# Softmax attention followed by a leaky-ReLU feed-forward: score chunks of 128 keys with a shared rest, loaded and scored one unit at a time

## The chip, the core and the metric

The kernel runs on one core of a Trainium2 chip. The core has TensorE (PE, matrix products; PEld is its weight load), VectorE (DVE), ScalarE (ACT), GpSimd (POOL) and SyncE (SP), each with its own in-order queue, and 16 DMA engines. Here SP and POOL issue nearly all transfers: SP the transposing DMAs and the stores, POOL the loads. The metric is the device time of one execution in microseconds (us); lower is better.

## The reference

Attention over 8 batches and 12 heads, 448 tokens, head size 64; the heads are joined to rows of 768; then two weight matrices with a leaky ReLU between them.

```
scores = scale * np.matmul(q, k.transpose(0, 1, 3, 2))        # 448 x 448 for each head
scores = scores - np.max(scores, axis=-1, keepdims=True)
attn   = np.exp(scores); attn = attn / (np.sum(attn, axis=-1, keepdims=True) + 1e-09)
x      = np.matmul(attn, v)                                     # then heads joined: 3584 x 768
h      = x @ w_in                                               # 768 -> 2048
out    = np.maximum(0.01 * h, h) @ w_out                        # 2048 -> 768
```

## The kernel before, in words

A **unit** is two heads of one batch: 48 units, six to a batch. For a unit, the keys lie on partitions in four chunks of 112. A **score chunk** (`scores`, lines 280-290) is two matmuls of 64 rows by 448 queries, one for each head, into one of three PSUM slots; `expo` (line 294) turns both heads' scores of that chunk into exponentials in one ACT instruction of 112 x 896. A **burst** (`burst`, lines 822-832) is three chunks in a row, six matmuls for the three slots, whatever units they belong to. **Rows** (`rows`, lines 793-816) are the product of a unit's exponentials with its values: 4 query blocks x 4 key chunks x 2 heads = 32 matmuls of 65 columns (64 values and a column of ones that gives the softmax's sum), then a reciprocal and a multiplication on DVE (lines 808, 809), then a transposing DMA of x on SP into `xT` (`x_transposes`, line 251).

Queries and keys come as pairs of units by one POOL load for q, k and v each (`load_soft`, line 143, 112 partitions x 4 heads x 256 elements, cast to bf16 on the way), are copied by POOL into `qkb` (`cast`, line 172; values into `v`, line 174), and from unit 15 on are turned by a transposing DMA on SP (`turn`, line 251) into `qkT`, which has four buffers. `qkb` and `e` have three buffers, `v` four.

The feed-forward works on seven stretches of tokens (`cuts`, line 41). For stretch i, `hidden` (lines 458-536, matmuls at line 483) makes the first layer by a scheme with mixed operands (`x_mix`, made on DVE at line 430 from `xT`, and `w_in_mix`), with partial sums kept in the pool `c`; `second(i)` (lines 941-973, matmuls at lines 555 and 620) makes the second layer. Between the steps of `second(i)` the function `place` (lines 885-939) puts bursts and rows, by a small model of when ACT is done and the slots are free (0.8 us for each exponential). `plan` (line 882) says how many bursts go into each `second(i)`, and `need` (line 44) which units must have had their rows before `hidden(i + 1)`; the DVE steps of `x_mix` for the next stretch are set in 7.0 model microseconds after the rows that they need. Two banks `g` take the second layer's sums, and DVE moves them out (lines 560, 563, 623). `advance` (lines 771-791) issues, in each step, the next turn on SP, the next casts on POOL and every second time a load.

All order is fixed when the kernel is built: every engine runs its list in order and waits on semaphores.

Of the kernel before, what the change touches and what calls it, by code (L numbers as in the profile page):

```python
# [16 lines left out]
def kernel(  # L17
# [19 lines left out]
    NW = DM // 2  # L37
    NU = B * HP
    scale = 1.0 / float(D) ** 0.5

# [8 lines left out]
    w_pool = ctx.enter_context(tc.tile_pool(name="weights", bufs=1))  # L49
    ld_pool = ctx.enter_context(tc.tile_pool(name="ld", bufs=2))  # L50
    cast_pool = ctx.enter_context(tc.tile_pool(name="cast", bufs=3))
    v_pool = ctx.enter_context(tc.tile_pool(name="vones", bufs=1))
# [29 lines left out]
    PL = D + 2  # L82
    v_sb = [v_pool.tile([SC, 2, NSC, VL], BF16, name=f"v{i}") for i in range(NV)]

    NE = 3
    EL = 2 * NSC * S
    e_sb = [exp_pool.tile([SC, EL + P - SC], BF16, name=f"e{i}") for i in range(NE)]


    NQ = 4  # L90
    QL = 2 * S
    qkT = [qk_pool.tile([P, QL + P - SC], BF16, name=f"qkT{i}") for i in range(NQ)]

# [30 lines left out]
    for t, n in ((h_mix, 2), (w_in_mix, 9), (w_mix, 9)):  # L124
        t = t.rearrange("p x k n -> p (x k n)")
        for j in range(n):
            rooms.append(t[:SC, ts(j, 4 * NSC * D)].bitcast(F32).rearrange("p (h so d) -> p h so d", h=2, so=NSC))

    def room(x):

        return rooms.pop(0) if rooms else ld_pool.tile([SC, 2, NSC, D], F32, name="f" + "qkv"[x])

    def half(t, i=None):

        t = t.rearrange("p h so d -> p (h so d)").bitcast(BF16)
        t = t.rearrange("p (u h so d) -> p u h so d", u=2, h=2, so=NSC)
        return t if i is None else t[:, i]

    def load_soft(u, n, which):
        b, hp = divmod(u, HP)  # L140
        for x in which:
            t = room(x)
            nc.gpsimd.dma_start(
                out=half(t)[:, :n].rearrange("p u h so d -> p (u h) (so d)"),
                in_=(q, k, v)[x][b, 2 * hp:2 * hp + 2 * n].rearrange(
                    "h (p so) d -> p h (so d)", so=NSC),
            )
            for i in range(n):
                raw.setdefault(u + i, {})[x] = half(t, i)

    def load_one(u, x, queue):
        b, hp = divmod(u, HP)
        t = room(x)
# [10 lines left out]
    def cast(u, parts=(0, 1, 2), by=nc.gpsimd.tensor_copy):  # L164
        if u >= NU:
            return
        for x in parts:
            f = raw[u].pop(x)
            if x < 2 and u not in qk_sb:
                qk_sb[u] = cast_pool.tile([SC, 2, NSC, 2, D], BF16, name="qkb")  # L170
            if x < 2:
                by(qk_sb[u][:, x].rearrange("p so h d -> p h so d"), f)  # L172
            else:
                by(v_sb[u % NV][:, :, :, :D], f)  # L174
    w_steps = []
# [56 lines left out]
    for t in e_sb:  # L232
        nc.vector.memset(t[:, EL:], 0.0)
    for t in qkT:
        nc.vector.memset(t[:, QL:], 0.0)
    fast = nc.vector.tensor_copy
# [12 lines left out]

    def turn(dst, src):  # L250
        nc.sync.dma_start_transpose(out=dst.rearrange("p (c s) -> p c s", s=SC), in_=src)
# [9 lines left out]
    def transposes(u, bank=None):  # L261
        if u >= min(NPE, NU):
            return
        for parts in ((1,), (0,)) if u == 0 else ((0, 1),):
            tr = turn_tile(bank)
            for i in parts:
                for so in range(NSC):
                    nc.tensor.transpose(  # L268
                        tr[:, i, ts(so, SC)], qk_sb[u][:, i, so], ident[:SC, :SC]
                    )  # L270
# [7 lines left out]
    sc_t = {}  # L278

    def scores(u, c):  # L280
        ps = next_slot()
        t = qkT[u % NQ]
        sc_t[u, c] = ps
        for j in range(2):
            nc.tensor.matmul(  # L285
                ps[:, j, :S],
                t[j * D:(j + 1) * D, S + c * SC:S + c * SC + P],
                t[j * D:(j + 1) * D, :S],
                start=True, stop=True,
            )  # L290

    def expo(u, c):
        e = e_sb[u % NE][:, :EL].rearrange("p (j c s) -> p j c s", j=2, c=NSC)
        nc.scalar.activation(e[:, :, c, :], sc_t.pop((u, c))[:SC, :, :S], AX.Exp, scale=scale)  # L294

    def pv(u, j, bank=None):
# [4 lines left out]
        for qc in range(NSC):  # L301
            for c in range(NSC):
                at = (j * NSC + c) * S + qc * SC
                nc.tensor.matmul(  # L304
                    ps[:, qc, :D + 1], e[:, at:at + P], vt[:, j, c, :D + 1],
                    start=(c == 0), stop=(c == NSC - 1),
                )
# [458 lines left out]
    chunk = 4 * HP + 3  # L766
    rows_done = HP
    to = {"pe": HP + 2, "turn": NPE, "q": HP + 4, "cast": HP + 4, "v": HP + 4, "load": [HP + 8] * 3}
    tick = 0

    def advance():
        nonlocal tick
        tick += 1
        u = to["turn"]
        if u < min(NU, chunk // NSC + NQ, to["cast"]):
            dma_transposes(u)
            to["turn"] += 1
# [15 lines left out]
    def rows():  # L793
# [3 lines left out]
        ps = next_slot()[:, :, :NSC * PL].rearrange("p j (q d) -> p j q d", q=NSC)  # L797
        for j in range(2):
            for qc in range(NSC):
                for c in range(NSC):  # L800
                    at = (j * NSC + c) * S + qc * SC
                    nc.tensor.matmul(  # L802
                        ps[:, j, qc, :D + 1], e[:, at:at + P], vt[:, j, c, :D + 1],
                        start=(c == 0), stop=(c == NSC - 1),
                    )
        x_t[u] = x_pool.tile([SC, NSC, 2, D], BF16, name="x")
        rec = r_pool.tile([SC, 2, NSC, 1], F32, name="rec")
        nc.vector.reciprocal(rec, ps[:SC, :, :, D:D + 1])  # L808
        nc.vector.tensor_mul(  # L809
            x_t[u].rearrange("p q j d -> p j q d"), ps[:SC, :, :, :D], rec.to_broadcast([SC, 2, NSC, D])  # L810
        )
        if u in X_PE:
# [9 lines left out]
    def burst(lazy=0):  # L822
        nonlocal chunk
        todo = [divmod(chunk + x, NSC) for x in range(3) if chunk + x < NU * NSC]
        assert rows_done > todo[-1][0] - NE and turned(todo[-1][0]) and to["v"] > rows_done
        for a, c in todo:
# [54 lines left out]

    plan = [9, 8, 8, 8, 8, 5, 0]
    model = {"now": 0.0, "act": 0.0, "free": {}, "ready": {}}

    def place(i, want, soon=0, full=True, calm=True, first=False, lazy=0, keen=NU, cap=NU):
# [3 lines left out]
        while True:  # L889
            settle_x(model["now"])  # L890
            now = model["now"]
            last = divmod(chunk + 2, NSC)[0]
            blocked = rows_done <= min(last, NU - 1) - NE
            u = rows_done
            whole = u < chunk // NSC
            at = [free.get(id(x), 0.0) for x in slots]
            u = to["pe"]
            if full and max(want, soon) > done and u <= min(last, NPE - 1) and state == 0:
# [4 lines left out]
                continue  # L903
            if want > done and state < 2 and turned(last) and not blocked and len(slots) == 3 and all(
                x <= now + 0.05 + 0.2 * j for j, x in enumerate(at)
# [8 lines left out]
                for x, t in enumerate(order[:chunk - start]):  # L914
                    model["act"] = max(model["act"], now + 0.45 + 0.2 * x) + 0.8
                    free[id(t)] = model["act"] + (0.3, 0.15 + 0.5 * (lazy > 1), 0.15 + 0.5 * lazy)[x]
                    if (start + x) % NSC == NSC - 1:
                        ready[(start + x) // NSC] = model["act"] + 0.1
                model["now"] = now + 0.78
                continue  # L920
            u = to["pe"]
            if first and full and state == 0 and u < min(NPE - 1, to["cast"] - 1) and u <= chunk // NSC + 1 and model["act"] <= now + 0.6:
# [6 lines left out]
            if calm and whole and not (lazy and late) and at[0] <= now + 0.05 and ready.get(u, 0) <= now + 0.05 and (  # L929
                u <= (chunk + 5) // NSC - NE or u < keen  # L930
            ) and u < cap:
# [9 lines left out]
    def second(i):  # L941
# [27 lines left out]
        assert left == 0 or chunk == NU * NSC, (i, left)  # L969
        assert i + 1 == NR or rows_done >= need[i + 2], (i, rows_done)  # L970
# [65 lines left out]
```

## Time and profile before

| | us |
|---|---|
| three runs: median (lowest to highest) | 388.05 (386.12 to 391.76) |
| the profiled execution's own time | 387.23 |
| its span (first to last instruction) | 385.4 |
| PE busy | 375.7 (97%) |
| ACT busy | 264.2 (69%) |
| DVE busy | 234.1 (61%) |
| POOL busy | 141.7 (37%) |

The span is what the profile divides its shares by; the 1.8 us by which the execution's own time is longer lie around it. An engine's busy time counts its own instructions; matmuls are pipelined and their ends modelled, so what one really costs is read from start to start of neighbours, not from its mean duration. In the answers below a line of the timeline gives the start, the time to the end of the last one, engine, line, operation, tiles and how many; in brackets how long the engine sat idle before it and what released it.

### The profile page before, as it was taken

The page shows a single profiled execution, that of the slowest core. Times are in us where ns is not written, and L with a number is a line of the kernel's source. Part 1 is how long each engine was busy: PE and PEld are TensorE (multiplying, and loading weights), DVE is VectorE, ACT ScalarE, POOL GpSimd, SP SyncE. Part 2 cuts the span into 40 slices and gives each one's busy share as a digit, 9 for nine tenths or more (in the row PEclk, how much of TensorE's full clock was granted, in tenths as well). Part 3 has the DMA queues.
Part 4 walks back from the last instruction along what each step waited for, and adds up shares of the span by engine and source line. Part 5 has one row for each costly group of instructions (what it writes and reads, how often), then busy time and mean ns, then how long its engine had stood idle before and what let it go on. Part 6 is the DMA issues. An engine that isn't in the chain of part 4 may idle for free.

```text
span 385.4 us, 10023 instructions
## 1 busy us (share of the span) xinstructions
PE 375.7 (97%) x4095; PEld 260.0 (67%) x4095; DVE 234.1 (61%) x488; ACT 264.2 (69%) x391; POOL 141.7 (37%) x223
## 2 busy tenths in 40 slices
PE   8999989999999999999999999999999999999995
PEld 3664646866488655886568865678655895668753
DVE  3663656775666746757459574566745665474753
ACT  5996874865768777687775877767776687717700
POOL 5998660764655443440436304353042100000000
PEclk9999999999999999999999999999999999999999
DMA  8999999899989948991499913999229600330022
GB/s 160 181 195 202 179 193 204 95 135 179 166 149 124 153 72 156 194 156 26 65 182 189 138 26 54 181 173 164 29 46 180 144 13 3 107 80 27 3 83 82
DMA packets 93278, 47.09 MB, mean 122 GB/s; under 512 B 51888, under 2 KB 89904, under 8 KB 93232
## 3 DMA queue, kind: packets, MB, share of 16 engines
q0 software_dynamic: 37536, 22.24, 45.5%
q1 hardware_dynamic: 55056, 23.66, 32.0%
q8 instruction: 32, 0.52, 0.6%
q10 hardware_dynamic: 640, 0.56, 0.5%
q14 instruction: 14, 0.11, 0.1%
HBM read 45.61 MB, written 11.01 MB: 147 GB/s over the span
## 4 chain that ended last, share of the span: by engine, by line
PE 90%; ACT 4%; DMA 2%; DVE 1%; issue 1%; ACTq 0%; DVEq 0%
PE g L555 30%; PE g L483 14%; PE sc L483 14%; PE sc L285 10%; PE sc L802 10%; PE g L366 3%; ACT e L294 3%; PE g L620 3%; PE g L662 2%; DMA xT<-x 2%; PE g L268 1%; DMA hmix<-in_k_dram 1%; PE g L304 1%; PE sc L366 1%; PE g L331 0%
## 5 line engine op out<-in xcount | busy, mean ns | idle before, releaser
L294 ACT ACTIVATE e<-sc 112x896 bf16<-112x896 f32 x192 | 162.7, 920 | 47.7 <-PE sc L285 47.7
L555 PEld LDWEIGHTS <-h 128*128 128x128 bf16 x632 | 57.2, 98 | 45.4 <-issue 13.7
L555 PE MATMUL g<-w_out_sb,h 128*128 128x384 bf16 x416 | 81.0, 326 | 0.0
L472 ACT ACTIVATE h<-c 128x512 bf16<-128x512 f32 (+1 forms) x72 | 43.5, 611 | 25.8 <-DVE c L498 17.4
L483 PEld LDWEIGHTS <-w_in_sb 128*128 128x128 bf16 x576 | 54.3, 98 | 5.9
L285 PE MATMUL sc<-qkT 64*128 64x448 bf16 x384 | 50.0, 355 | 1.4 <-ACT e L294 0.6
L172 POOL COPY qkb<-fq 112x512 bf16<-112x512 bf16 x38 | 25.4, 668 | 68.8 <-DMA qkT<-qkb 33.7
L174 POOL COPY v<-fv 112x512 bf16<-112x512 bf16 x38 | 24.6, 660 | 69.2 <-PE sc L802 69.2
L802 PEld LDWEIGHTS <-e 112*128 112x128 bf16 x1344 | 46.2, 97 | 5.0 <-ACT e L294 0.8
L802 PE MATMUL sc<-v,e 112*128 112x65 bf16 x1344 | 47.6, 193 | 0.4 <-ACT e L294 0.4
L483 PEld LDWEIGHTS <-w_in_mix 128*128 128x128 bf16 x432 | 41.2, 98 | 4.1
L560 DVE COPY o<-g 128x384 f32<-128x384 f32 x49 | 27.1, 554 | 21.6 <-PE g L555 21.3
L555 PE MATMUL g<-w_mix,h 128*128 128x384 bf16 (+1 forms) x208 | 38.3, 323 | 0.9 <-DVE o L563 0.9
L285 PEld LDWEIGHTS <-qkT 64*128 64x128 bf16 x384 | 15.6, 94 | 28.3 <-issue 19.5
L172 POOL COPY qkb<-fk 112x512 bf16<-112x512 bf16 x38 | 25.8, 678 | 19.4 <-DMA fk<-in_k_dram 19.4
L808 DVE RECIPROCAL rec<-sc 112x8 f32<-112x8 f32 x42 | 8.7, 207 | 39.2 <-PE sc L802 39.1
L563 DVE TENSOR_TENSOR o<-o,g 128x384 f32<-128x384 f32 x39 | 21.5, 552 | 17.4 <-PE g L555 15.6
L809 DVE TENSOR_TENSOR x<-sc,rec 112x512 bf16<-112x512 f32 x42 | 29.0, 691 | 1.4
L483 PE MATMUL g<-xT,w_in_sb 128*128 128x256 bf16 (+1 forms) x216 | 28.5, 268 | 0.0
L483 PE MATMUL sc<-xT,w_in_sb 128*128 128x256 bf16 (+1 forms) x216 | 28.5, 268 | 0.0
L555 PE MATMUL g<-w_mix,hmix 128*128 128x384 bf16 x104 | 20.1, 326 | 0.0
L366 PE MATMUL g<-xT,w_in_sb 128*128 128x448 bf16 x84 | 18.7, 353 | 1.3 <-ACT h L642 1.3
(106 smaller groups left out, 478.5 us busy)
## 6 DMA issues: line engine op xcount, KB each, us to landing
fq<-in_q_dram POOLq DMA_DIRECT2D x19, 224.0 KB, 5.6
fk<-in_k_dram POOLq DMA_DIRECT2D x19, 224.0 KB, 7.0
fv<-in_v_dram POOLq DMA_DIRECT2D x19, 224.0 KB, 5.7
w_in_sb<-in_moe_w_in_dram POOLq DMA_DIRECT2D x4, 768.0 KB, 11.3
w_out_sb<-in_moe_w_out_dram POOLq DMA_DIRECT2D x4, 768.0 KB, 19.2
out_dram<-o SPq DMA_DIRECT2D x7, 336.0 KB, 4.7
out_dram<-o SPq DMA_DIRECT2D x8, 288.0 KB, 4.0
out_dram<-o SPq DMA_DIRECT2D x7, 240.0 KB, 3.7
```

Source lines behind the costliest of these rows:

```text
L172: by(qk_sb[u][:, x].rearrange("p so h d -> p h so d"), f)
L174: by(v_sb[u % NV][:, :, :, :D], f)
L285: nc.tensor.matmul(ps[:, j, :S], t[j * D:(j + 1) * D, S + c * SC:S + c * SC + P], t[j * D:(j + 1) * D, :S], start=True, stop=True,)
L294: nc.scalar.activation(e[:, :, c, :], sc_t.pop((u, c))[:SC, :, :S], AX.Exp, scale=scale)
L366: nc.tensor.matmul(open_t[m][:, :n], w_in_sb[:, kk, ts(m, P)], xT[:, kk, at:at + n], start=(fresh and kk == kks[0]), stop=(kk == KD - 1),)
L472: nc.scalar.activation(hs[:, m:m + 2, cols], x.rearrange("p (m t) -> p m t", m=2), AX.Prelu, alpha=0.01)
L483: nc.tensor.matmul(ps[:, j * nh:(j + 1) * nh], w[:, kk, ts(j, P)], x[:, kk], start=(first and j == 0 and kk == 0), stop=(kk == KH - 1), sk ...
L555: nc.tensor.matmul(ps[:, cols], x[:, m], w[:, m], start=(first and m == 0), stop=(m == MH - 1), skip_group_check=True,)
L560: by(o[:, at], ps[:, :NW])
L563: nc.vector.tensor_add(o[:, at], o[:, at], ps[:, :NW])
L802: nc.tensor.matmul(ps[:, j, qc, :D + 1], e[:, at:at + P], vt[:, j, c, :D + 1], start=(c == 0), stop=(c == NSC - 1),)
L809: nc.vector.tensor_mul(x_t[u].rearrange("p q j d -> p j q d"), ps[:SC, :, :, :D], rec.to_broadcast([SC, 2, NSC, D]))
```

## The change

From unit 18 on (`WIDE`), the keys of a unit are three chunks of 128 and a rest of 64. A burst is then exactly one unit's three chunks. The rest of both heads shares one matmul: the 128 partitions of `qkT` hold both heads' d, and its last 128 columns hold head 0's 64 rest keys over zeros for head 1, and head 1's 64 over zeros for head 0; one exponential of 128 x 448 follows (`rest`). Rows are 4 query blocks x (2 heads x 3 chunks of 65 columns + one matmul of 130 columns for the rest) = 28 matmuls. In the whole kernel the score matmuls go from 384 to 324 of the paired kind and 30 of the shared kind, and those of `rows` from 1344 of 65 columns to 1104 of 65 and 120 of 130.

Keys and values of a pair of units are loaded by three POOL transfers instead of one (128 partitions x 4 heads x 192 elements, then two of 64 partitions x 2 units x 64 elements), 60 more in all, with 19 memsets on POOL for the zeros; the turns of these units take 128 rows instead of 112. `qkb` and the landing tiles become named buffers in a fixed rotation, as many as before. The pool `c` has four buffers instead of five. `place` sets a unit's rest as soon as a slot is free after its burst, and no next burst before it; `hidden` sets a rest that is still owed. `plan` has 8, 7, 6, 6, 6, 3 bursts instead of 9, 8, 8, 8, 8, 5.

```diff
+    WIDE = 3 * HP
+    NWC = S // P
+    REST = S - NWC * P
...
-    c_pool = ctx.enter_context(tc.tile_pool(name="c", bufs=5))
+    c_pool = ctx.enter_context(tc.tile_pool(name="c", bufs=4))
...
+    qkb = [cast_pool.tile([P, 2 * NSC, 2, D], BF16, name=f"qkb{i}") for i in range(3)]
...
+    def load_wide(u, x):
+        b, hp = divmod(u, HP)
+        t = room(x).rearrange("p h so d -> p (h so d)").bitcast(BF16)
+        t = t.rearrange("p (u h so d) -> p u h so d", u=2, h=2, so=NSC)
+        src = (q, k, v)[x][b, 2 * hp:2 * hp + 4]
+        nc.gpsimd.dma_start(
+            out=t[:, :, :, :NWC].rearrange("p u h so d -> p (u h) (so d)"),
+            in_=src[:, :NWC * P].rearrange("h (p so) d -> p h (so d)", so=NWC),
+        )
+        for j in range(2):
+            own, other = (slice(y * REST, (y + 1) * REST) for y in (j, 1 - j))
+            if u < WIDE + 4:
+                nc.gpsimd.memset(t[other, :, j, NWC], 0.0)
+            nc.gpsimd.dma_start(out=t[own, :, j, NWC], in_=src[j::2, NWC * P:].rearrange("u r d -> r u d"))
+        for i in range(2):
+            raw.setdefault(u + i, {})[x] = t[:, i]
...
     def load_soft(u, n, which):
         b, hp = divmod(u, HP)
         for x in which:
+            if x > 0 and u >= WIDE:
+                load_wide(u, x)
+                continue
...
     def dma_transposes(u):
         if NPE <= u < NU:
-            turn(qkT[u % NQ][:, :QL], qk_sb[u].rearrange("p i so h d -> p (i so h d)"))
+            rows_of, s = (P, P) if u >= WIDE else (SC, SC)
+            turn(qkT[u % NQ][:, :2 * NSC * s], qk_sb[u][:rows_of].rearrange("p so h d -> p (so h d)"), s)
...
+    def rest(u):
+        ps = next_slot()[:, 0, :S]
+        nc.tensor.matmul(ps, qkT[u % NQ][:, (2 * NSC - 1) * P:2 * NSC * P], q_of(u), start=True, stop=True)
+        at = 2 * NWC * S
+        nc.scalar.activation(e_sb[u % NE][:, at:at + S], ps, AX.Exp, scale=scale)
...
+            for qc in range(NSC):
+                b, y = divmod(2 * qc, NSC)
+                for j in range(2):
+                    for c in range(NWC):
+                        at = (j * NWC + c) * S + qc * SC
+                        nc.tensor.matmul(
+                            ps[:, b, y + j, :D + 1], e[:, at:at + P], vt[:, j, c, :D + 1],
+                            start=(y + j + c == 0), stop=False, skip_group_check=True,
+                        )
+                at = 2 * NWC * S + qc * SC
+                nc.tensor.matmul(
+                    ps[:, b, y:y + 2, :D + 1], e[:, at:at + P], vt[:, :, NWC, :D + 1],
+                    start=False, stop=True, skip_group_check=True,
+                )
...
-    plan = [9, 8, 8, 8, 8, 5, 0]
+    plan = [8, 7, 6, 6, 6, 3, 0]
...
+            if calm and owed_rest and at[0] <= now + 0.05:
+                t = slots[0]
+                u = set_rest()
+                model["act"] = max(model["act"], now + 0.25) + 0.5
+                free[id(t)] = model["act"] + 0.15
+                ready[u] = model["act"] + 0.1
+                model["now"] = now + 0.19
+                continue
...
-            if step % 4 == 2 and NSC * (rows_done + 1) <= chunk:
+            if step % 4 == 2 and owed_rest:
+                set_rest()
+            elif step % 4 == 2 and rows_done < scored():
                 rows()
```

More of the change, by code (lines that the diff above doesn't have):

```diff
@@ L82 @@
     PL = D + 2
-    v_sb = [v_pool.tile([SC, 2, NSC, VL], BF16, name=f"v{i}") for i in range(NV)]
+    v_sb = [v_pool.tile([P, 2, NSC, VL], BF16, name=f"v{i}") for i in range(NV)]
     NE = 3
     EL = 2 * NSC * S
-    e_sb = [exp_pool.tile([SC, EL + P - SC], BF16, name=f"e{i}") for i in range(NE)]
+    e_sb = [exp_pool.tile([P, EL + P - SC], BF16, name=f"e{i}") for i in range(NE)]
     NQ = 4
     QL = 2 * S
-    qkT = [qk_pool.tile([P, QL + P - SC], BF16, name=f"qkT{i}") for i in range(NQ)]
+    qkT = [qk_pool.tile([P, 2 * NSC * P], BF16, name=f"qkT{i}") for i in range(NQ)]
+    qkb = [cast_pool.tile([P, 2 * NSC, 2, D], BF16, name=f"qkb{i}") for i in range(3)]
     NX = 15 * P
@@ L169, in cast @@
             if x < 2 and u not in qk_sb:
-                qk_sb[u] = cast_pool.tile([SC, 2, NSC, 2, D], BF16, name="qkb")
+                qk_sb[u] = qkb[u % len(qkb)]
+            so = slice(x * NSC, x * NSC + f.shape[2])
+            if x == 0 and WIDE <= u < WIDE + len(qkb):
+                nc.gpsimd.memset(qk_sb[u][96:, :NSC], 0.0)
             if x < 2:
-                by(qk_sb[u][:, x].rearrange("p so h d -> p h so d"), f)
+                by(qk_sb[u][:f.shape[0], so].rearrange("p so h d -> p h so d"), f)
             else:
-                by(v_sb[u % NV][:, :, :, :D], f)
+                by(v_sb[u % NV][:f.shape[0], :, :f.shape[2], :D], f)
+            if x == 2 and WIDE <= u < WIDE + NV:
+                for j in range(2):
+                    nc.gpsimd.memset(v_sb[u % NV][(1 - j) * REST:(2 - j) * REST, j, NWC, D:D + 1], 0.0)
     w_steps = []
@@ L278, with q_of @@
     sc_t = {}
+    def q_of(u):
+        s = P if u >= WIDE else SC
+        return qkT[u % NQ][:, :NSC * s].rearrange("p (so s) -> p so s", s=s)[:, :, :SC]
     def scores(u, c):
@@ L767, with at_chunk, scored, set_rest @@
     rows_done = HP
+    owed_rest = []
+    total = WIDE * NSC + (NU - WIDE) * NWC
+    def at_chunk(x):
+        return divmod(x, NSC) if x < WIDE * NSC else (WIDE + (x - WIDE * NSC) // NWC, (x - WIDE * NSC) % NWC)
+    def scored():
+        return owed_rest[0] if owed_rest else at_chunk(chunk)[0]
+    def set_rest():
+        u = owed_rest.pop(0)
+        rest(u)
+        return u
     to = {"pe": HP + 2, "turn": NPE, "q": HP + 4, "cast": HP + 4, "v": HP + 4, "load": [HP + 8] * 3}
@@ L823, in burst @@
         nonlocal chunk
-        todo = [divmod(chunk + x, NSC) for x in range(3) if chunk + x < NU * NSC]
-        assert rows_done > todo[-1][0] - NE and turned(todo[-1][0]) and to["v"] > rows_done
+        todo = [at_chunk(chunk + x) for x in range(3) if chunk + x < total]
+        assert rows_done > todo[-1][0] - NE and turned(todo[-1][0]) and to["v"] > rows_done and not owed_rest
+        if todo[0][0] >= WIDE:
+            assert todo[0][1] == 0
+            owed_rest.append(todo[0][0])
         for a, c in todo:
@@ L903, in place @@
                 continue
-            if want > done and state < 2 and turned(last) and not blocked and len(slots) == 3 and all(
+            if want > done and state < 2 and turned(last) and not blocked and not owed_rest and len(slots) == 3 and all(
                 x <= now + 0.05 + 0.2 * j for j, x in enumerate(at)
@@ L916, in place @@
                     free[id(t)] = model["act"] + (0.3, 0.15 + 0.5 * (lazy > 1), 0.15 + 0.5 * lazy)[x]
-                    if (start + x) % NSC == NSC - 1:
-                        ready[(start + x) // NSC] = model["act"] + 0.1
+                    if at_chunk(start + x + 1)[1] == 0 and not owed_rest:
+                        ready[at_chunk(start + x)[0]] = model["act"] + 0.1
                 model["now"] = now + 0.78
@@ L921, in place @@
             u = to["pe"]
-            if first and full and state == 0 and u < min(NPE - 1, to["cast"] - 1) and u <= chunk // NSC + 1 and model["act"] <= now + 0.6:
+            if first and full and state == 0 and u < min(NPE - 1, to["cast"] - 1) and u <= scored() + 1 and model["act"] <= now + 0.6:
                 transposes(u)
```

74 lines of the change are left out of this document (43 added, 31 removed).

## The prediction

> **What bounds the kernel now.** First the page's busy times, the slices and the chain that ended last:
>
> ```profile
> PE 375.7 (97%) x4095; PEld 260.0 (67%) x4095; DVE 234.1 (61%) x488; ACT 264.2 (69%) x391; POOL 141.7 (37%) x223
> ...
> PEclk9999999999999999999999999999999999999999
> ...
> PE 90%; ACT 4%; DMA 2%; DVE 1%; issue 1%; ACTq 0%; DVEq 0%
> ```
>
> PE carries the chain at full clock. So the stretches, to see where it is not full:
>
> ```profile
> 70.00:98.00 28.00, 28.00 (x337) 18.02 (x336) 18.72 (x36) 18.90 (x26) 18.11 (x27) 1.00 1.13 140
> 98.00:107.00 9.00, 8.13 (x81) 4.22 (x80) 6.64 (x14) 6.39 (x8) 4.87 (x7) 1.00 1.37 180
> 107.00:128.00 21.00, 21.00 (x237) 18.67 (x236) 14.92 (x27) 15.90 (x29) 12.43 (x20) 1.00 0.91 132
> 128.00:156.00 28.00, 28.00 (x288) 15.84 (x287) 15.20 (x32) 20.89 (x27) 10.11 (x17) 1.00 0.88 128
> ```
>
> (Each row: the stretch, its length, then busy PE, PEld, DVE, ACT, POOL with counts, clock, DMA share, GB/s.) From 107 to 363 us PE is busy in every stretch. Before, it loses 2.6 us of the first 20, 2.2 of 20 to 70, 0.9 around 105; at the end 4.0 of 22.4. So the change gains by fewer PE nanoseconds alone, and loses by any wait that PE does not have now. The PE timeline gives prices from start to start:
>
> ```profile
> 98.09 0.49 PE L555 MATMUL g<-w_out_sb,h 128*128 128x384 bf16 x2
> 98.52 0.74 PE L285 MATMUL sc<-qkT 64*128 64x448 bf16 x6
> 99.19 1.15 PE L555 MATMUL g<-w_out_sb,h 128*128 128x384 bf16 x6
> 100.17 1.14 PE L802 MATMUL sc<-v,e 112*128 112x65 bf16 x32
> 101.15 1.14 PE L555 MATMUL g<-w_mix,hmix 128*128 128x384 bf16 x6
> 102.22 0.74 PE L285 MATMUL sc<-qkT 64*128 64x448 bf16 x6
> ```
>
> Burst: 99.19 - 98.52 = 0.67. Six matmuls at line 555 take 0.98 ahead of rows but 1.07 ahead of a burst (101.15 to 102.22): a burst costs some 0.10 more, 0.77 in all. Rows: 0.98. Last, the chain at its one DMA piece, and the queues there:
>
> ```profile
> 98.68 5.84 DMA xT<-x
> ```
>
> ```profile
> 96.57 2.02 SPq L251 DMA_TRANSPOSE qkT<-qkb  x1
> 98.68 1.29 SPq L251 DMA_TRANSPOSE xT<-x  x1
> ```
>
> ```profile
> 79.18 0.62 POOL L172 COPY qkb<-fq 112x512 bf16<-112x512 bf16 x1
> ...
> 95.09 0.61 POOL L172 COPY qkb<-fk 112x512 bf16<-112x512 bf16 x1 [2.65 <-DMA fk<-in_k_dram]
> ```
>
> x of unit 16 was ready near 95.9, but its turn stood on SP behind the turn of unit 20, which waited for POOL's key copy, which waited for a load. It landed at 104.5; DVE sat 1.81 us on it ahead of line 430, and PE 0.87 behind DVE. That is the only place where the load chain reaches PE, and the change lengthens this chain.
>
> **Part by part.**
>
> *Bursts.* From the early part on 55 bursts become 45: 10 x 0.77 = 7.7 us less on PE. *Rests:* 30 matmuls of 448 columns; the nearest row is line 366, 128 x 448, six from 41.64 to 42.78: 0.19 each, 5.7 us. The upper bound is 0.29, if each pays the burst's 0.10 too (8.7); it runs over all 128 rows as its neighbours do, so I take 0.19. The lower bound is nothing, if it ran wholly beside others; line 366 shows no such overlap.
>
> *Rows.* The columns stay (32 x 65 = 24 x 65 + 4 x 130 = 2080). A matmul of 65 costs 0.98 / 32 = 30.6 ns; a column, by line 555, 0.163 us / 384 = 0.42 ns. One of 130 is then 55 to 61 ns, rows 0.96 to 0.98. If the count set the price it would be 0.98 x 28/32 = 0.86. I take 0.965: 30 x 0.015 = 0.5 less. **PE work: -7.7 + 5.7 - 0.5 = -2.5 us.**
>
> *ACT.* Three exponentials take 2.53 us (843 ns each; columns, not partitions, set it, so 128 costs as 112 did); the rest's is nearest to line 642, 128 x 448, 548 ns. 30 x (3.37 - 2.53 - 0.55) = 9 us less, covered by ACT's idle 31%. But `place` counts 0.8 and 0.5: rows set right behind their rest can come 3 x 0.04 + 0.05 = 0.2 early. One or two in each of five second layers: 0 to 2 us, and I take 0.5.
>
> *POOL.* 60 more load issues at 0.70 (line 143) are 42 us, 19 memsets at most 0.6 each (a copy's price), say 4 us: POOL at 188 us, not a bound. What counts is what stands behind them. The copies of unit 16 at 79.18 get four more issues and four memsets ahead of them, 2.8 to 5 us. Their turn was issued at 80.45 and landed at 86.28; the burst that needs it began at 86.75. As that landing took 5.8 us with transfers ahead of it and a lone turn takes 2.9 (139.32 to 142.24), much of the delay is eaten in the queue: 0 to 4, I take 0.5. The key copy of unit 20 gets six issues ahead of it, 4.2 us and some memsets, against POOL's idle 2.99 at 81 to 84 us that can absorb part: 1.8 to 4.8 later. The turn of x behind it on SP was already late, so DVE and PE get it nearly in full where it is not absorbed. I take the low end, **+1.8 us** at this boundary.
>
> *SP.* The turns take 128 rows for 112, one seventh more bytes. From the third second layer on the x of the last unit that the next `hidden` needs stands behind one more key turn than before (units come every burst, so SP's turns move up): 1.2 to 1.9 us of SP (the turns at 192.74 and 194.81 took 1.97 and 1.78), besides the 2.8 us of four issues that POOL spends on a pair's keys and values. Before, the next-to-last x landed at 199.85 and line 430 began at 203.42: 3.6 us of cover. 1.9 + 2.8 - 3.6 = 1.1 us uncovered at each of four boundaries: **+4.4 us** (bounds 0, if POOL's issues lie in its idle time, and 4.7 each, without cover). What is queued behind line 430 on DVE are the copies that empty the two banks `g`: PE stops one or two products later.
>
> *DMA engines.* A wide load has the same bytes in 4 x 128 + 256 = 768 pieces for 448. Queue 0 shows 45.5% x 16 x 385.4 / 37536 = 75 ns a packet, 592 bytes on average: 448 x 75 / 16 = 2.1 us of all engines. By bytes it stays 2.1, by pieces 3.6. Queue 1, mostly packets under 512 bytes, shows 32.0% x 16 x 385.4 / 55056 = 36 ns, so I take 2.6: 30 x 0.5 = 15 us over some 240 us at a share of 0.2 to 1.4. That is covered except near 105 us (counted above). The Trainium skill, "DMA: Bandwidth & Descriptors", Specifications, says that pieces under 512 bytes fall below line rate because the engine reads, modifies and writes; the new pieces are 384 and 128 bytes at the target. Queue 1's 36 ns do not show it; with it the load would go by pieces, as in the second rival.
>
> *At nothing:* four buffers `c` (a buffer's last reader and its next writer are both ACT, in order); the named `qkb` and landing buffers (as many as before); the new memsets on DVE (before its first work).
>
> Sum: -2.5 + 0.5 + 0.5 + 1.8 + 4.4 = +4.7. Against the profiled execution's 387.23 that is 391.9; it lies 0.8 under the median of the three, whose scatter is 5.6. **Forecast 392 us**: PE's small gain is more than given back where `hidden` waits for x.
>
> **Rivals.**
>
> *All covered.* For it: PE waits for a DMA nowhere between 107 and 363 us, and POOL has 63% idle. Against it: the boundary at 105 us has no cover at all. -2.5 + 0.5 = 385.2 us. Chance 0.12.
>
> *The load chain sets the pace (slower).* Keys by pieces (3.6 us a load) and POOL in order: keys come late, SP's turns wait for them, x behind them. It decides when the key copies fall more than about 4 us behind, the cover above. Then each of the four boundaries costs up to 4.7 and the first up to 4.8 more, and units whose turns landed just ahead of their burst (unit 26: 150.40 for 153.9) add 1 to 3 each: half of this 398, all of it 410. For it: four of the five waits that I priced stand on this one chain. Against it: DMA share 0.33 and less from 302 us on, and POOL's idle time. Chance 0.40.
>
> *Rests and rows cheaper than their columns (faster).* Rests hidden, rows by count: -7.7 - 30 x 0.12 = -11.3, 376 us. Against it: line 366. Chance 0.05.
>
> The forecast itself, some wait at the boundaries up to +8: 0.43.
>
> **How the numbers follow.** Two per cent, about what a measurement of this kernel can tell from no change, is 7.7 us. Same: 0.43 + 0.12 = 0.55; slower 0.40; faster 0.05. The range goes from 385, the covered case (0.05 to 0.08 lie under it), to 403, some two thirds of the way through the slower rival (0.12 above). Its own range for the forecast is 386 to 396.
>
> **What would show it.** In the changed profile: a burst from start to start still 0.67 and a rest 0.19; rows 0.96; ACT some 9 us less busy; POOL near 188 us. The stretches from 107 us on would show PE short by 1 to 2 us at the starts of `hidden`, with DVE's line of `x_mix` idle before it and DMA xT<-x as its releaser. If PE is full there, the covered case holds; if the burst's weight load waits for DMA qkT<-qkb inside the second layers, the load chain does. I am wrong altogether if a rest or rows cost PE more than their columns, or if the loads' pieces cost more than 75 ns.

## The result and the profile after

| | before | after |
|---|---|---|
| 20 runs each, side by side: median (lowest to highest), us | 387.52 (386.03 to 391.76) | 390.35 (388.54 to 394.37) |
| the profiled execution's own time, its span, us | 387.23, 385.4 | 388.54, 386.7 |
| PE, ACT, POOL busy, us | 375.7, 264.2, 141.7 | 373.6, 252.4, 184.4 |

The ratio is 1.0088 (95% interval 1.0067 to 1.011): slower by less than one per cent. A second set of runs gave 1.0058 (1.0037 to 1.0079); one execution in it had a mean granted clock of 0.656 and took 540 us, is left out, and its profile is not read. The profiled execution of after is the fastest of its 20, so its profile shows the least of what the others lose.

The page of after, its busy times and its chain:

```profile
PE 373.6 (97%) x3945; PEld 259.1 (67%) x3945; DVE 234.1 (61%) x491; ACT 252.4 (65%) x391; POOL 184.4 (48%) x302
...
PE 81%; DMA 6%; DVE 5%; ACT 4%; issue 3%; POOL 0%; DVEq 0%; ACTq 0%
```

PE has 2.1 us less to do, and yet it carries 81% of the chain instead of 90%: DMA and DVE have taken its place. The stretches (columns as before):

```profile
98.00:107.00 9.00, 9.00 (x86) 5.14 (x85) 6.90 (x15) 7.05 (x10) 7.20 (x17) 1.00 1.06 160
107.00:128.00 21.00, 20.55 (x226) 18.13 (x224) 13.46 (x26) 14.41 (x27) 10.46 (x21) 1.00 0.98 125
128.00:156.00 28.00, 27.74 (x265) 15.40 (x264) 15.79 (x30) 20.11 (x28) 21.75 (x34) 1.00 1.09 141
248.00:258.00 10.00, 8.63 (x81) 5.45 (x80) 4.67 (x12) 5.07 (x8) 4.21 (x7) 1.00 1.08 125
```

Before, PE was full from 107 to 363 us; now it lacks 0.45, 0.26 and 1.37 us in three of these rows. The prices on the PE timeline of after:

```profile
189.30 0.74 PE L330 MATMUL sc<-qkT 64*128 64x448 bf16 x6
189.98 1.15 PE L612 MATMUL g<-w_out_sb,h 128*128 128x384 bf16 x6
190.96 0.35 PE L349 MATMUL sc<-qkT 128*128 128x448 bf16 x1
191.15 1.46 PE L612 MATMUL g<-w_mix,h 128*128 128x384 bf16 x8
```

A burst is 189.98 - 189.30 = 0.68, a rest 191.15 - 190.96 = 0.19 (0.189 is the median of all 30); rows of the new form have a median of 0.963 ahead of first-layer products and 0.972 ahead of second-layer ones, read in the same way. Where PE stopped at 255 us, the chain of after reads (start, length, what):

```profile
245.20 0.04 DVE x L900
...
246.64 7.96 DMA xT<-x
254.61 0.02 issue
254.63 0.30 DVE x_mix L487
254.94 0.02 issue
254.96 0.29 DVE xT L487
255.25 0.47 DVE o L620
255.73 0.04 issue
255.77 0.81 PE g L540 x6
```

The last `x` that `hidden` needs was multiplied out by 245.9, its turn was issued at 246.64, and it took 7.96 us to land. DVE's `x_mix` waited, behind it on DVE the addition that empties a bank `g` (line 620), and behind that PE. What ran beside that turn is in the transfers of 244 to 256 us, before and then after (tile, queue, count, size of one, median us from issue to landing):

```profile
fq<-in_q_dram POOLq DMA_DIRECT2D x1, 224.0 KB, 4.4
fk<-in_k_dram POOLq DMA_DIRECT2D x1, 224.0 KB, 5.9
...
xT<-x SPq DMA_TRANSPOSE x2, 2.5
```

```profile
fq<-in_q_dram POOLq DMA_DIRECT2D x1, 224.0 KB, 5.6
fk<-in_k_dram POOLq DMA_DIRECT2D x1, 192.0 KB, 7.4
...
fk<-in_k_dram POOLq DMA_DIRECT2D x2, 16.0 KB, 6.9
xT<-x SPq DMA_TRANSPOSE x1, 8.0
```

The same loads stand in both. Before, they were issued at 247.74 and 249.54, behind the last turns of x (245.69 and 246.99); after, at 245.01 and 246.64, ahead of it and with it. The turn of x went out at about the same time in both (246.99 and 246.64), so what differs is its landing. POOL copies unit 41's keys only when the turn of unit 38 has freed their buffer. After, that turn goes out earlier (239.43 for 242.08), and all that POOL has queued behind the copy moves up with it. In all, `x_mix` waits:

```profile
DVE x_mix L487 <- DMA xT<-x: 8.4, 5, 2.5
```

(us, times, longest; before: 1.8, once.)

To see where PE lost time, take each `hidden` from its first to its last matmul start on PE, and the second layer behind it from there to the next `hidden` (the last columns: hidden 5 and its second layer). The row "lowest" has the lowest value of each column in any profile of a kernel of the changed kind below; as every value includes all the work, it is an upper bound on what the work alone takes.

| us | h1 | s1 | h2 | s2 | h3 | s3 | h4 | s4 | h5 | s5 | sum |
|---|---|---|---|---|---|---|---|---|---|---|---|
| before | 20.27 | 28.57 | 20.18 | 28.57 | 20.19 | 28.57 | 20.18 | 28.57 | 15.73 | 26.09 | 236.92 |
| after | 20.94 | 29.62 | 21.21 | 27.54 | 21.12 | 28.72 | 21.11 | 27.11 | 16.67 | 24.85 | 238.89 |
| lowest | 20.16 | 29.05 | 21.12 | 27.11 | 21.12 | 27.11 | 21.11 | 27.11 | 16.66 | 24.85 | 235.40 |
| holdqk (below) | 20.16 | 29.90 | 21.12 | 27.11 | 21.12 | 27.48 | 21.11 | 27.12 | 16.67 | 24.85 | 236.64 |

So the work here is at least 1.5 us shorter than before, and even this fastest execution gave back 3.5: 0.8 in h1, 0.6 in s1, 0.4 in s2 and 1.6 in s3.

### The profile page after: what moved, and what is told of

Same layout as the page of the kernel before. It is cut to its first block, busy times and chain, and to the rows that moved or that the text cites. A ratio compares the mean times of both kernels' runs of the same rounds, so it can differ in the third digit from the quotient of the medians.

```text
span 386.7 us, 9815 instructions
## 1 busy us (share of the span) xinstructions
PE 373.6 (97%) x3945; PEld 259.1 (67%) x3945; DVE 234.1 (61%) x491; ACT 252.4 (65%) x391; POOL 184.4 (48%) x302
## 3 DMA queue, kind: packets, MB, share of 16 engines
q0 software_dynamic: 48096, 22.24, 50.5%
## 4 chain that ended last, share of the span: by engine, by line
PE 81%; DMA 6%; DVE 5%; ACT 4%; issue 3%; POOL 0%; DVEq 0%; ACTq 0%
PE g L612 25%; PE g L540 13%; PE sc L540 13%; PE sc L330 8%; PE sc L888 5%; DMA xT<-x 4%; ACT e L344 3%; PE g L423 3%; PE g L677 3%; PE sc L877 3%; PE g L719 2%; PE sc L893 2%; PE sc L349 1%; DMA hmix<-in_k_dram 1%; PE g L307 1%
## 5 line engine op out<-in xcount | busy, mean ns | idle before, releaser
L344 ACT ACTIVATE e<-sc 128x896 bf16<-128x896 f32 (+1 forms) x162 | 137.5, 922 | 44.8 <-PE sc L330 44.8
L612 PEld LDWEIGHTS <-h 128*128 128x128 bf16 x632 | 58.7, 98 | 47.9 <-issue 12.9
L330 PE MATMUL sc<-qkT 64*128 64x448 bf16 x324 | 42.5, 353 | 1.6 <-ACT e L344 0.6
L205 POOL COPY qkb<-fk 128x512 bf16<-128x512 bf16 (+1 forms) x38 | 26.7, 704 | 22.7 <-DMA fk<-in_k_dram 22.7
L888 PEld LDWEIGHTS <-e 128*128 128x128 bf16 x720 | 30.3, 97 | 4.0 <-ACT e L344 2.3
L888 PE MATMUL sc<-v,e 128*128 128x65 bf16 x720 | 32.1, 193 | 0.2 <-DVE x L900 0.2
L207 POOL COPY v<-fv 128x512 bf16<-128x512 bf16 (+1 forms) x38 | 25.1, 675 | 14.8 <-PE sc L893 14.8
L330 PEld LDWEIGHTS <-qkT 64*128 64x128 bf16 x324 | 12.7, 94 | 24.3 <-issue 16.8
L893 PE MATMUL sc<-v,e 128*128 128x130 bf16 x120 | 26.7, 222 | 0.0
L552 ACT COPY c<-g 128x512 f32<-128x512 f32 (+1 forms) x12 | 6.8, 568 | 22.8 <-PE g L540 22.8
```

The lines of the kernel that those rows point to most:

```text
L205: by(qk_sb[u][:f.shape[0], so].rearrange("p so h d -> p h so d"), f)
L207: by(v_sb[u % NV][:f.shape[0], :, :f.shape[2], :D], f)
L330: nc.tensor.matmul(ps[:, j, :S], t[j * D:(j + 1) * D, k0:k0 + P], q_of(u)[j * D:(j + 1) * D] if u >= WIDE else t[j * D:(j + 1) * D, :S], s ...
L344: nc.scalar.activation(e[:, :, c, :], sc_t.pop((u, c))[:e.shape[0], :, :S], AX.Exp, scale=scale)
L612: nc.tensor.matmul(ps[:, cols], x[:, m], w[:, m], start=(first and m == 0), stop=(m == MH - 1), skip_group_check=True,)
L888: nc.tensor.matmul(ps[:, b, y + j, :D + 1], e[:, at:at + P], vt[:, j, c, :D + 1], start=(y + j + c == 0), stop=False, skip_group_check=True,)
```

## The experiments

Two theories of why x lands late, and one rival to both. **O**: its place on SP, behind key turns (the term priced at 4.4 us). **L**: the loads of queries and keys that run beside its turn. **P**: the 60 small transfers as such. All runs are compared with the kernel before on the same chip; each had 12 timed runs, xfirst 6, holdqk_norest 13.

**The changed kernel again** (no edit).

> The changed kernel unchanged, beside the three others on the same chip, for a second profile of it. Its runs so far lie between 388.5 and 394.4 us, the kernel before's between 386.0 and 391.8, so nearly 3 us between the medians. If the extra time is waits for x at the boundaries (both theories of the waits), a profile of a slower execution shows the same 2.2 us less PE work and more than the 3.0 us of PE idle gaps beyond 4.5 that the first profile of it has, at the starts of hidden. If it is a fixed price on PE (the rival that rests or rows cost more than read), the idle gaps stay and PE's busy time is larger.

Ratio 1.0058, the other eleven runs at 388.3 to 394.4 us. There is no second profile to read, so this says only that the loss and its scatter are real.

**Key turns held until the last x is out** (O).

```diff
-        if u < min(NU, scored() + NQ, to["cast"]):
+        if u < min(NU, scored() + NQ, to["cast"]) and (rows_done >= last or u < last + 2):   # last = need[i + 2]
```

> In second layers, the turns of keys two units and more past the last unit that the next hidden needs are held back until that unit's x has been issued. Theory O (order on SP: x stands behind key turns, the term priced at 4.4 us): the last x goes out 1.3 to 4 us earlier at the later boundaries, the waits of x_mix for DMA xT<-x (8.4 us on DVE, 5 times) nearly vanish, and the median falls by 2 to 4 us, to 386 to 388. Theory L (the loads of queries and keys share the DMA engines with that turn): the turn still lands 5 to 8 us after its issue where a load runs beside it; the time falls by 0 to 1.5 us. Theory P (PE work): no change.

397.5 us, ratio 1.0227 (1.0183 to 1.0271). The wait of `x_mix` did fall, to 2.8 us, once; but now bursts waited for the key turns, by the waits and the PE timeline of xfirst:

```profile
PEld L330 <- DMA qkT<-qkb: 12.5, 5, 4.8
```

```profile
158.80 0.74 PE L330 MATMUL sc<-qkT 64*128 64x448 bf16 x6 [4.46 <-DMA qkT<-qkb]
```

The edit held too much and tells little of O; it shows that the key turns cannot be held back that long. order1 below is the gentler form.

**All loads held near the boundary** (L).

```diff
-        if tick % 2 == 0:
+        if tick % 2 == 0 and loads:       # loads = rows_done < need[i + 2] - 2, in each second layer
```

> In second layers, no load is issued from the rows of the last unit but two that the next hidden needs until hidden begins; the loads come some 8 us later, the order on SP stays nearly as it is. Theory L (the last x lands late, 5.8 us and 8.0 us after its issue at 199 and 247 us against 2.5 to 3.2 before, because the pair's loads of queries and keys, which were issued behind it in the kernel before, now run beside it): it lands 2.4 to 3.5 us after its issue, the waits of x_mix fall from 8.4 to under 3 us, and the median falls by 2 to 4 us, to 386 to 388. Theory O (order on SP): x goes out at the same place, so at most 1 us is gained. If the loads are then late for their copies, bursts wait for DMA qkT<-qkb and it gets slower by more than 1 us.

387.9 us, ratio 1.0007 (0.9983 to 1.003), 2.4 under the changed kernel. The wait of `x_mix` fell to 1.7 us, and s2 and s3 took 27.11 and 27.44. The landing did not come out as expected: 6.3 and 5.8 us, as POOL does not wait for `hidden` and ran on into the next loads of values and queries. That the wait shrank all the same fits the margin. From the landing to `hidden`'s first product some 1.2 us pass (254.61 to 255.77 in the chain above), and here the turn went out 7.8 and 8.0 us ahead of that product, so that 6.3 and 5.8 us just fit. In the changed kernel and in the next run it went out 7.8 us ahead of where PE stopped; their 8.0 and 7.3 us do not fit, and PE stops for 1.37 and 1.39 us. But at 149 us PE stopped for 2.1 us, for another reason than a late key turn, and the clock fell behind it (last section): s1 was 33.19 us.

**The small loads left out** (P).

```diff
-                nc.gpsimd.memset(t[other, :, j, NWC], 0.0)
-            nc.gpsimd.dma_start(out=t[own, :, j, NWC], in_=src[j::2, NWC * P:].rearrange("u r d -> r u d"))
+                nc.gpsimd.memset(t[:, :, j, NWC], 0.0)
```

> The two loads of the 64 rest keys and values of a pair are left out (60 issues on POOL, 9600 pieces); their places stay zero, so the rest's products run over zeros. PE, ACT and DVE run the same instructions. If the small transfers cause the lateness (by POOL's 0.6 us each or by their pieces on the DMA engines): POOL busy falls by 36 us to about 148, the x turns land 2 to 3 us after their issue, the median falls by 2.5 to 4.5 us, to 386 to 388. If only the order and the timing of the large loads count: within 1 us of the changed kernel's 390.4.

388.0 us, ratio 1.0013 (0.9984 to 1.0042). By its time, P would have won. Its profile (an execution of 389.9) says otherwise of the boundaries: in the transfers of 245 to 257 us,

```profile
fq<-in_q_dram POOLq DMA_DIRECT2D x1, 224.0 KB, 6.6
fk<-in_k_dram POOLq DMA_DIRECT2D x1, 192.0 KB, 7.2
...
xT<-x SPq DMA_TRANSPOSE x1, 7.3
```

x still lands after 7.3 us without any small load, and s2 and s3 are no shorter than in the changed kernel (28.78, 28.91). Its h1 and s1 are at their lowest (20.16, 29.05). From h1 to s5 this execution takes 239.0 us, as long as the changed kernel's profile, so where the 2.4 us of the median came from is not seen in it. The interval of this ratio just overlaps that of the changed kernel run again (1.0037 to 1.0079). By the time, P is likely a cause besides, but not the one behind x's late landing.

**Loads of queries and keys alone held, at the two later boundaries** (L).

```diff
-            x = min(range(3), key=lambda x: to["load"][x])
+            x = min(kinds, key=lambda x: to["load"][x])
...
-                    advance()
+                    advance((2,) if 2 <= i < NR - 1 and rows_done >= need[i + 2] - 2 else (0, 1, 2))
...
-            advance()
+            advance((2,) if i > 2 and rows_done <= need[i + 1] < NU else (0, 1, 2))
```

> The changed kernel, but from the third second layer on no load of queries or keys is issued from the rows of the last unit but two that the next hidden needs until that hidden has had one unit's rows (the loads of units 36 and 42); loads of values stay, and the two earlier boundaries are left as they are. Theory L (loads beside the last x's turn): at 200 and 250 us that turn lands 2.4 to 4 us after its issue instead of 5.8 and 8.0, PE does not stop at 255 us (1.37 us in the changed kernel's profile), and no burst waits for a key turn at 150 us as with all loads held (2.1 us of PE and 3.4 us at a granted clock of 0.5 to 0.7 behind it); the median falls to 386 to 387.5, some 3 us under the changed kernel. If the turn is late by its place on SP, the median stays above 389. If bursts of units 36 or 42 wait for their turns: above 389 as well, with those waits in the list.

387.6 us, ratio 0.9986 (0.9959 to 1.0013): 2.7 us under the changed kernel's median, and the intervals of the two ratios don't meet. s2 and s3 are at 27.11 and 27.48, as the table above shows, and PE's gap at 255 us is 0.20. In the transfers of 244 to 256 us of holdqk:

```profile
fv<-in_v_dram POOLq DMA_DIRECT2D x1, 192.0 KB, 5.8
...
qkT<-qkb SPq DMA_TRANSPOSE x3, 6.1
...
xT<-x SPq DMA_TRANSPOSE x1, 5.3
```

The turn took 5.3 us for 8.0 (4.2 for 5.8 at 199 us), with a pair's values beside it (three issues) in place of its queries and keys (four): less of a gain than L foresaw, but enough.

**Sixty small loads added to the kernel before** (P), with its products unchanged and c at four buffers:

```diff
+            if x > 0 and u >= 3 * HP:
+                small.append(small.pop(0))
+                for j in range(2):
+                    nc.gpsimd.dma_start(
+                        out=small[-1][j * 64:(j + 1) * 64],
+                        in_=(q, k, v)[x][b, 2 * hp + j:2 * hp + 4:2, 384:].rearrange("u r d -> r u d"),
+                    )
```

> The kernel before, with four buffers for c (the room is needed) and with 60 more loads of 64 partitions x 2 x 64 elements into tiles that nothing reads, two behind each key and value load from unit 18 on; the products are the kernel before's. POOL busy rises by some 36 us. If the small transfers cost the changed kernel its time (the run without its rest loads was 2.4 us faster): 1.5 to 3.5 us slower than before, near 390. If what costs is the order in which large loads meet the turns of x, which this keeps: within 1 us of before.

388.3 us, ratio 1.002 (0.9995 to 1.0045): 0.8 us, with the interval just across no change, and under the 1.5 to 3.5 that P asked for. POOL was 177.0 us busy, as foreseen.

**Four buffers for c in the kernel before.**

```diff
-    c_pool = ctx.enter_context(tc.tile_pool(name="c", bufs=5))
+    c_pool = ctx.enter_context(tc.tile_pool(name="c", bufs=4))
```

> The kernel before with four buffers for the pool c instead of five, nothing else. The prediction put this at nothing: within 0.6 us of before, and no new wait of ACT at the copies into c. If a fifth buffer matters, PE would wait for ACT or DVE in hidden, at each of six: 1 to 3 us slower.

387.4 us, ratio 0.9998 (0.9973 to 1.0024), and every `hidden` as long as before to 0.01 us: nothing, as predicted.

**holdqk without the small loads** (the diffs of holdqk and norestload).

> The kernel of the run holdqk, without the two loads of the rest keys and values of a pair (their places stay zero), as in norestload. If the two causes are separate and each gives 2.4 to 3 us of the changed kernel's time back: 384.5 to 385.5, the time that the PE work alone gives (387.5 less 2.2). If both stand for one cause (x's turns meet fewer transfers), no faster than the better of the two: 386.5 to 388.

386.5 us, ratio 0.9963 (0.9948 to 0.9979), 1.15 under holdqk and 3.9 under the changed kernel. By the medians the two causes add, though not fully (2.7 and 2.4 each alone). The intervals of the two ratios overlap, and the one profile, of this kernel's slowest execution (388.5), does not show where the 1.15 came from.

**One key turn behind the last x instead of ahead of it** (O, the gentle form).

```diff
-        if u < min(NU, scored() + NQ, to["cast"]):
+        if u < min(NU, scored() + NQ, to["cast"]) and (rows_done >= last or u < last + 4):   # last as above, from the second second layer on
```

> The changed kernel with one edit on SP: in the second layers from the second on, the key turn of the fourth unit past the last one that the next hidden needs goes out behind that unit's x instead of ahead of it, and no other key turn moves far. Loads are not touched. In the changed kernel's profile x stood on SP 1.9, 0.75 and 1.4 us behind its multiplication at 197, 246 and 295 us. If the place on SP is what makes x late: 1 to 2 us faster than the changed kernel, 388 to 389. If the loads beside the turn are what counts: x goes out 1 to 1.5 us earlier, but still lands 5 to 7 us later, and the median stays within 0.8 us of 390.4.

390.0 us, ratio 1.0075 (1.0036 to 1.0113): no change. In the transfers of 246 to 258 us the turn of x went out 0.03 us after the multiplication (0.34 at 200 us) and still landed 5.3 us after its issue (7.25 at 200 us), beside

```profile
fq<-in_q_dram POOLq DMA_DIRECT2D x1, 224.0 KB, 5.3
fk<-in_k_dram POOLq DMA_DIRECT2D x1, 192.0 KB, 5.3
...
xT<-x SPq DMA_TRANSPOSE x1, 5.3
```

In its one profile s2 and s3 are shorter than the changed kernel's (27.39, 27.74), but s1 is 30.64: what it may give at two boundaries it loses at another. The changed kernel itself has the opposite case. Here are its transfers of 296 to 298 us, where no load is left:

```profile
qkT<-qkb SPq DMA_TRANSPOSE x1, 3.8
xT<-x SPq DMA_TRANSPOSE x1, 2.5
```

This x stood 1.4 us behind key turns and had one beside it, yet it landed in 2.5 us, and s4 is at its lowest. O as the main cause falls; a part of 1 us at single boundaries is not excluded.

**The two edits together** (the diffs of holdqk and order1).

> The edits of holdqk and order1 together. If place on SP and loads add up: 1 us under holdqk's 387.6, near 386.5. If with the loads out of the way x has slack: the same as holdqk within 0.6 us.

388.3 us, ratio 1.0026 (0.9991 to 1.0062): nothing beyond holdqk.

**The load of values held as well** (the diff is against holdqk).

```diff
-        if tick % 2 == 0:
+        if tick % 2 == 0 and kinds:
...
-                    advance((2,) if 2 <= i < NR - 1 and rows_done >= need[i + 2] - 2 else (0, 1, 2))
+                    advance((0, 1, 2) if i < 2 or i + 1 == NR or rows_done < need[i + 2] - 2 else (2,) if rows_done < need[i + 2] else ())
...
-            advance((2,) if i > 2 and rows_done <= need[i + 1] < NU else (0, 1, 2))
+            advance(() if i > 2 and rows_done <= need[i + 1] < NU else (0, 1, 2))
```

> holdqk, and the load of values that follows the last needed rows held back as well, until hidden has had one unit's rows; in holdqk's profile it ran beside the last x's turn, which took 4.2 and 5.3 us. Theory L: that turn lands 2.4 to 3.5 us after its issue, x_mix's wait at 200 and 250 us vanishes; 0 to 1 us under holdqk, 386.5 to 387.6. If values then come late in hidden: rows or POOL wait for DMA fv, and it is slower than holdqk.

388.0 us, ratio 1.0018 (0.9989 to 1.0047), s2 and s3 27.12 and 27.31: no better than holdqk.

**One boundary more** (the diff is against holdqk).

```diff
-                    advance((2,) if 2 <= i < NR - 1 and rows_done >= need[i + 2] - 2 else (0, 1, 2))
+                    advance((2,) if 1 <= i < NR - 1 and rows_done >= need[i + 2] - 2 else (0, 1, 2))
...
-            advance((2,) if i > 2 and rows_done <= need[i + 1] < NU else (0, 1, 2))
+            advance((2,) if i > 1 and rows_done <= need[i + 1] < NU else (0, 1, 2))
```

> holdqk with the loads of queries and keys held one boundary earlier too (the loads of unit 30 at the second layer that ends near 156 us). In the changed kernel's profile DVE waited 1.68 us for x there and PE lost some 0.6 us in that second layer. Theory L: that second layer falls from 29.6 us to 29.0 to 29.3, the rest as in holdqk; the median is 0.3 to 1 us under holdqk's, 386.6 to 387.3, and under the kernel before. If unit 30's and 32's turns come late in the next second layer: bursts wait there, and it is above 388.

387.6 us, ratio 0.9998 (0.9976 to 1.002); s1 was 30.12 and not 29.0 to 29.3. So what s1 loses (0.6 to 1.6 us in most of these kernels) does not come from these loads. The small loads are a candidate: norestload's one profile does not lose it, and small, on the kernel before, has an s1 of 29.09 for 28.57. But holdqk_norest, without small loads, has 29.94. What it comes from stays open.

Of versions that compute the whole result, holdqk is the fastest by its ratio; it takes back the loss and does not beat the kernel before.

## Why the prediction came out as it did

*The total* (392 against 390.35; +4.7 against +2.8) and the likeliest case, PE's small gain given back and more where `hidden` waits for x, were right. That the sum came so near is in part luck: the 2.3 us priced at unit 16's turn and at the first boundary did not arise, while some 2 us came from places that were not priced (the small transfers, and what stays open in h1 and s1). The signature was as described: PE short at the starts of `hidden`, DVE idle before `x_mix`, its releaser DMA xT<-x.

*Bursts, rests, rows*: 0.674, 0.189 and 0.963 us from start to start, for 0.67, 0.19 and 0.965. The sum of -2.5 was -2.1 by PE's busy time, and -1.5 by the table from the first `hidden` on; three of the five pairs of stages give the -0.5 each that the terms make. *ACT* fell by 11.8 us and not 9: the term was made with 843 ns from start to start, while the records of the large exponentials, old and new, are 917 ns long, and the rest's 565; 30 x (0.917 - 0.565) is 10.6, and 1.2 are left open. It was covered, as said.

*POOL* 184.4 us (188 forecast); small issues took 0.59 to 0.66, the memsets 0.1 to 0.5. *Unit 16's turn* was priced at 0.5 and cost nothing: PE is full from 70 to 98 us after as before. *The first boundary* was priced at +1.8. There the step failed that says x gets POOL's lateness nearly in full. The key copy of unit 20 was 1.24 us later (96.33 for 95.09), its turn 0.66 (97.23 for 96.57) but shorter on SP (1.34 for 2.02), and x went out at 98.67 for 98.68. POOL's idle time took part of it; before, the turn had stood on SP behind stores until 96.47 us, and it was shorter now, which took the rest. The gap of 0.87 at 105 us is gone (c4, which keeps all but the pool, does not have it either); instead h1 loses 0 to 1.3 us from kernel to kernel, with the same work in it, 0.8 in the changed kernel's profile.

*SP*, +4.4 at four boundaries: the sign was right, the place at the ends of s2 and s3 but not of s4 and s5, and the cause was wrong. x did stand behind key turns, by 1.9, 0.75 and 1.4 us at 197, 246 and 295 us (1.2 to 1.9 were forecast), but order1 shows that this is not what decided. The step that failed is "That is covered except near 105 us", under *DMA engines*: the loads were counted by the work they bring, which was right (queue 0 went from 45.5% to 50.5% of 16 engines, 3125 - 2806 = 319 us, or 319 / 16 / 30 = 0.66 us of all engines a load, for 0.5), and not by when they start. The last turn of x took 4 to 8 us beside loads in these runs, and 2.5 with none in flight (296 us). The key turns, which the prediction itself had moving up with the bursts, free the buffers earlier, and so set the loads beside that turn. The Trainium skill, "DMA: Bandwidth & Descriptors", Queues, rings and completion order, says that each DMA engine takes turns between its queues packet by packet; the 8.0 us beside four loads agree with that, though no run here separates it from other ways of sharing.

*The rival in which the load chain sets the pace* had the right agent and the wrong price: pieces cost 30 ns each (319 us over 10560 more packets), and not 75 or more, and keys came in time: in the whole profile of after a burst waits 0.2 us for a key turn. The rival *all covered* is nearly what holdqk_norest makes of it: 386.5 against 385.2.

Put together from the medians: 390.35, less 2.7 for the loads at two boundaries (holdqk), less 1.15 for the small transfers (holdqk_norest), leaves 386.5. From there to 387.5 - 1.9 = 385.6 (the work from 107 us on is 1.5 shorter by the table, that ahead of it some 0.4 by the prediction's prices for one burst less and two rests more) 0.9 stay unexplained, most likely in h1 and s1.

## What to carry to other kernels

Price a transfer that ends on the critical path by what runs beside it, not by its length when alone, and hold it against the margin that it has: look for the loads that your change sets in motion just ahead of it, and hold them until it has landed. Where every queue runs in order, an edit that frees a buffer earlier moves all that stands behind it, loads included; list that before counting bytes. And with PE 97% busy, a change that saves it 2 us was settled here only by laying the waits at each stage's start out next to the work.

## What the hardware showed that was not expected

In one run a row of copies on POOL stopped PE, and that short stop cost nearly twice its length. In hold, the loads held back came together, and so did POOL's copies from them. On the timelines of DVE and of POOL in hold:

```profile
144.24 3.84 DVE L624 TENSOR_TENSOR h<-h 128x1024 bf16<-128x1024 bf16 x1 [1.71 <-PE g L612]
```

```profile
144.14 0.63 POOL L205 COPY qkb<-fq 112x512 bf16<-112x512 bf16 x1
144.69 0.63 POOL L205 COPY qkb<-fk 128x512 bf16<-128x512 bf16 x1
145.25 0.62 POOL L205 COPY qkb<-fq 112x512 bf16<-112x512 bf16 x1
145.81 0.62 POOL L205 COPY qkb<-fk 128x512 bf16<-128x512 bf16 x1
146.36 1.16 POOL L207 COPY v<-fv 128x512 bf16<-128x512 bf16 x2
```

The instruction of DVE at line 624 takes 0.69 us at the median of 13; here it ended only behind the sixth copy. Behind it on DVE stood the multiplications of x that free the score slots, and so PE stopped for 1.63 and 0.48 us. The Trainium skill, "SBUF — State Buffer", SBUF: two separate sides, says that DVE (with two inputs in SBUF) and GpSimd share a pair of ports as an exclusive lock, and the loser waits for the other's whole instruction; that agrees, except that here DVE waited for six in a row. Other products of DVE with both inputs in SBUF were up to 0.5 us longer under a copy, before and after alike. Those with an input in PSUM were not: `x<-sc,rec` takes 0.69 us in after, from 100 us on, in 14 cases under a copy and in 17 without.

PE's stretches at that place (the third figure from the end is the granted clock):

```profile
148.00:150.00 2.00, 0.36 (x2) 0.10 (x2) 1.93 (x6) 0.94 (x2) 0.50 (x1) 1.00 1.11 371
150.00:152.00 2.00, 1.72 (x8) 0.84 (x8) 1.28 (x3) 1.65 (x2) 0.67 (x2) 0.71 1.37 123
152.00:154.00 2.00, 2.00 (x8) 0.94 (x7) 0.51 (x1) 0.54 (x1) 0.84 (x2) 0.50 1.00 215
154.00:156.00 2.00, 2.00 (x15) 0.79 (x13) 0.05 (x1) 0.71 (x1) 2.00 (x4) 0.93 0.16 32
```

The clock was at half for some 3.4 us (2.0 x 0.29 + 2.0 x 0.50 + 2.0 x 0.07 = 1.7 us lost, at half speed), which is nearly as much as the stop itself. The same followed the stop of 4.46 us in xfirst (clock 0.50 from 160 to 162 us), but not that of 2.75 us there at 259 us, nor the 1.37 at 255 us in the changed kernel. The Trainium skill, "TensorE: Matmul & The Clock Gate", Part 1, has two clock levels, half and full, and a free-running window of 3.4 us, an idle one of which brings the lower level. Levels and length agree with these rows; that a stop of 2.1 us in all was enough, and one of 2.75 us was not, goes beyond what that section of the Trainium skill states.
